# Normalised rows transposed by DMA instead of on TensorE, with stores and loads of v begun by ScalarE

## The chip, the cores and the metric

The kernel runs on one core of a Trainium2 chip. The core has five engines that work side by side, each with its own list of instructions: TensorE (PE, matrix products), VectorE (DVE), ScalarE (ACT), GpSimd (POOL) and SyncE (SP), which only begins DMA transfers. ScalarE and GpSimd can begin transfers too. The metric is the device time of one execution in microseconds (us), lower is better.

## What is computed

Attention with a causal mask and a decay from a cumulative sum of `s`, for 8 batches of 8 heads, 576 tokens and head width 64; then a layer norm over the 512 joined channels, a two-layer MLP of width 2048 with relu, and the residual sum.

```python
scores = scale * np.matmul(q, k.transpose(0, 1, 3, 2))
cum = np.cumsum(np.maximum(s, 0.0), axis=-1)
bias = -(cum[:, :, :, None] - cum[:, :, None, :])
scores = np.where(causal, -1e9, scores + np.minimum(bias, 0.0))
attn = softmax(scores)                      # over the last axis
x = np.matmul(attn, v)                      # heads joined: (8, 576, 512)
xn = (x - mean(x)) / np.sqrt(var(x) + 1e-6) * g_ln
out = x + np.maximum(xn @ w_ch1, 0.0) @ w_ch2
```

## The kernel before

The main loop runs over n = 0 to 63, one (batch, head) pair a step: b = n // 8, h = n % 8. The order of the instructions on each engine is that of the code (a manual schedule); semaphores are put in where data or a buffer is waited for.

A step n does this. `pre(n)` (L675) begins loads, casts and DMA transposes for later heads. `scores` (L304) multiplies keys by queries into three PSUM banks, and ScalarE takes the exponential of each (L323); from n = 10 on GpSimd then cuts the diagonal blocks to the causal triangle (L331). `scores_d` (L341) does the last 64 tokens for two heads at a time. `pv_next` (L729) multiplies the probabilities of the head two steps back by v (L389), and VectorE divides by the row sums (L397 to L406). Between these stand units of the MLP of the batch before: `run_units` (L557) takes them from a queue, 32 a batch. The first 16, `mlp1` (L493), make one block of 128 hidden channels each: four matmuls of 512 columns and a relu on ScalarE (L507), for the first unit of a step on VectorE (L505). The other 16, `mlp2` (L511), are quarters of the second layer for four tiles of 128 tokens; the last quarter is followed by VectorE's scaling and residual sum (L524) and a store (L542). A batch has a fifth piece, its last 64 tokens; these of two batches share a tile `xm`, and the four such tiles make a ninth, mixed set of units at the end.

Queries and keys come in two ways. For groups of four heads with a number below NPE (5 before, so heads up to 3 of batch 2) `ld_cast_pair` (L130) loads two heads by a casting DMA of GpSimd's, `qk_pair` (L275) transposes them on TensorE and VectorE and ScalarE copy them out of PSUM. Later groups are loaded as token rows: `ld_rows` (L159) in SyncE's queue, `cast_rows` (L172) on GpSimd, which also appends the bias columns, and `tr_rows` (L182), a DMA transpose in SyncE's queue. They run 6 to 2 steps ahead of the group's first head.

v of batches 2 to 7 is loaded by `ld_v` (L134, in SyncE's queue, one of five tiles a step at heads 1 to 5 of the batch before) and cast by GpSimd one step later (`cast_v`, L152). Row loads and v loads share the buffers of the pool `stage`, of which there are six.

The layer norm of a batch follows its last head, at head 1 of the next batch: `ln_xn` (L444) makes the rows minus mean times gain, `xn`, on VectorE, one tile after the other. `ln_tr` (L478) transposes a tile: four matmuls against the identity into PSUM and one copy into `xT` (or `xTm` for the mixed tile). For batches 1 to 6 that is at heads 2 and 3 of the next batch, between units. At the end of head 3 the next 32 units are queued; the first of them, at head 4, needs all four full tiles of `xT`.

SyncE's queue thus holds, in the order of the code, row loads, DMA transposes of rows, v loads and stores. Each DMA also waits until an earlier one has ended, the last that used the same one of eight semaphores.

Of the kernel before, what the change touches and what calls it, by code (L numbers as in the profile page):

```python
# [9 lines left out]
F32 = mybir.dt.float32  # L10
# [5 lines left out]
P = 128  # L16
# [3 lines left out]
def kernel(  # L20
# [25 lines left out]
    EW = 1664  # L46
    G = 4
    NG = BH // G
    NPE = 5
    NM = 10  # L50
    NR = 4
    QT = 6
    QP = S // QT

    const = ctx.enter_context(tc.tile_pool(name="const", bufs=1))
    stage = ctx.enter_context(tc.tile_pool(name="stage", bufs=6))
    pairs = ctx.enter_context(tc.tile_pool(name="pairs", bufs=4))
    small = ctx.enter_context(tc.tile_pool(name="small", bufs=4))
    xpool = ctx.enter_context(tc.tile_pool(name="xpool", bufs=3))
# [74 lines left out]
    def ld_v(b, t):  # L134
        if b >= B:
            return
        pn = P if t < NF else TL
        tmp = stage.tile([P, H, D], F32, name="vtmp", tag="st")
        nc.sync.dma_start(
            out=tmp[:pn], in_=v[b, :, t * P : t * P + pn, :].rearrange("h s d -> s h d")  # L140
        )
        loaded["v", b, t] = tmp
# [137 lines left out]

    def k_cols(b, h, kb):
        i, hh = (b * 2 + h // G) % 2, h % G
        if b * 2 + h // G < NPE:
            return kq[i][0:KA, 0, hh, kb * P : (kb + 1) * P]
        n = P if kb < NF else TL
        o = kb * 2 * G * P + hh * n
        return kq[i].rearrange("p u h s -> p (u h s)")[0:KA, o : o + P]

    def q_cols(b, h, q0, q1):
        i, hh = (b * 2 + h // G) % 2, h % G  # L290
        if b * 2 + h // G < NPE:
            return [(q0, q1, kq[i][0:KA, 1, hh, q0:q1])]
        flat = kq[i].rearrange("p u h s -> p (u h s)")
        full = flat[0:KA, 0 : NF * 2 * G * P].rearrange("p (t h s) -> p t h s", t=NF, s=P)
        o = NF * 2 * G * P + (G + hh) * TL
        got = []
        if q0 < NF * P:
            qf = min(q1, NF * P)
            got.append((q0, qf, full[:, q0 // P : qf // P, G + hh, :]))
        if q1 > NF * P:  # L300
            got.append((NF * P, q1, flat[0:KA, o : o + TL]))
        return got
# [175 lines left out]
    def ln_tr(b, t, eng="dve"):  # L478
# [9 lines left out]
            dst = xTm[:, :, (b // 2) * P : (b // 2 + 1) * P]  # L488
        copy_on(eng, dst, tr)

    first_unit = [False]

    def mlp1(xT, fb):  # L493
# [45 lines left out]
    def batch_units(b):  # L539
        def of_t(t):  # L540
            def put(yo, c0, c1):
                nc.sync.dma_start(out=out[b, t * P : (t + 1) * P, c0:c1], in_=yo)  # L542
            return xb[b][:, t, :], rstd[:, b, t : t + 1], put
        return chunk_units(lambda: xTs[b], of_t)

# [7 lines left out]

    queue = []
    pend = []

    def run_units(n, dve_first=False):  # L557
        for i in range(n):
            if queue:
                first_unit[0] = dve_first and i == 0  # L560
                queue.pop(0)()

# [103 lines left out]

    PAIR_LOADS = {11: 8, 12: 9}
    PAIRS = {9: 5, 11: 6, 13: 7, 14: 8, 15: 9}


    def pre(n):  # L675
        if n == 0:
            nc.vector.memset(mhalf, -0.5)
            ld_cast_pair(4)
        elif n == 1:
            ld_w1(1)  # L680
        elif n == 3:
            ld_cast_pair(5)
            for t in range(NT):
                ld_cast_v(1, t)
        elif n == 4:
            ld_w1(2)
            ld_w1(3)
        elif n == 7:
            ld_cast_pair(6)
            ld_w2(0)  # L690
            ld_cast_pair(7)
            ld_w2(1)
        elif n == 10:
            ld_w2(2)
            ld_w2(3)
        elif n == 12:
            nc.vector.memset(cT[:, :, 0, :, 0], -1.0)
            nc.vector.memset(cT[:, :, 1, :, 1:4], 1.0)
        elif n == 14:
            for r in rows:  # L700
                nc.gpsimd.memset(r[:, :, :, KA:P], 0.0)
        if n in PAIR_LOADS:
            ld_cast_pair(PAIR_LOADS[n])
        if n % 4 == 0 and 2 <= n // 4 + 1 < NPE:
            aug(n // 4 + 1, nc.sync)
        for gam in range(NPE, NG):
            m = n - 4 * gam
            if m == -6:
                ld_rows(gam, 0), ld_rows(gam, 1)
            elif m == -5:  # L710
                cast_rows(gam, 0), cast_rows(gam, 1)
                ld_rows(gam, 2), ld_rows(gam, 3)
            elif m == -4:
                tr_rows(gam, 0), tr_rows(gam, 1)
                cast_rows(gam, 2), cast_rows(gam, 3)
                ld_rows(gam, 4)
            elif m == -3:
                tr_rows(gam, 2), tr_rows(gam, 3)
                cast_rows(gam, 4)
            elif m == -2:  # L720
                tr_rows(gam, 4)
        for nb in range(2, B):
            m = n - H * nb + (5 if nb == 2 else 7)
            if 0 <= m < NT:
                ld_v(nb, m)
            if 1 <= m <= NT:
                cast_v(nb, m - 1, "pool")
# [17 lines left out]
    for n in range(BH):  # L745
        b, h = n // H, n % H
        pre(n)
        if n < 8:
            scores(b, h)
            if h in (1, 3, 5, 6):  # L750
                scores_d(b, h // 2)
            if h in (0, 2, 4):
                qk_pair(h // 2 + 1, ("dve", "dve"), ("act", "dve" if h < 4 else "act"))
            pend.append((b, h))
            if n == 7:
                pv_next()
                tr_pair(4)
                pv_next()
                evac_pair("k", 4, ("act", "act"))
                evac_pair("q", 4, ("act", "act"))  # L760
                trc = bias_tr()
                keep_warm(8)
                continue
            if n % 2 == 1 or n == 0:
                keep_warm(2)
            if n > 1:
                pv_next()
            if n == 6:
                pv_next()
            continue  # L770
        if n == 8:

            phs = [
                pool.tile([P, 512], F32, name="ph", tag=tag)
                for pool, tag in ((ps_m, "m"), (ps_m, "m"), (ps_s, "s"), (ps_s, "s"))
            ]

            def columns(t):
                cols = slice(t * P, (t + 1) * P)
                for fb, ph in enumerate(phs):  # L780
                    for kd in range(KD):
                        nc.tensor.matmul(
                            ph[:, cols],
                            lhsT=w1_bf[:, kd, fb * P : (fb + 1) * P],
                            rhs=xTs[0][:, kd, cols],
                            start=(kd == 0),
                            stop=(kd == KD - 1),
                        )

            for t in range(NF):  # L790
                ln_tr(0, t, "act" if t < 3 else "dve")
                if t > 0:
                    columns(t - 1)
            columns(NF - 1)
            for fb, ph in enumerate(phs):
                if fb % 2 == 0:
                    nc.scalar.activation(out=hT[:, fb, :], in_=ph, func=ACT.Relu)
                else:
                    nc.vector.tensor_scalar_max(out=hT[:, fb, :], in0=ph, scalar1=0.0)
            ln_first_rstd()  # L800
            queue += batch_units(0)[4:]
            scores(b, h)
            scores_d(b, h // 2)
            pend.append((b, h))
            run_units(1)
            continue

        end = next(m for m in (8 * i + 3 for i in range(2, B + 1)) if m >= n)
        nu = (2 if n < 16 else -(-len(queue) // (end - n + 1))) - 2
        if n in PAIRS:  # L810
            qk_pair(PAIRS[n], ("dve", "dve"), ("act", "act"))
        scores(b, h)
        run_units(1, True)
        if h % 2 == 0:
            scores_d(b, h // 2)
        run_units(1)
        if n > 9:
            pv_next()
        if n == 9:
            bias_rows(trc)  # L820
        pend.append((b, h))
        lt = {2: (0, 1), 3: (2, 3, 4)}.get(h, ()) if b > 1 else ()
        for t in lt:
            ln_tr(b - 1, t, "act" if b == 2 else "dve")
            if t != 1 and t != 4:
                run_units(1)
                nu -= 1
        if n == 2 * H + 2:
            for t in range(3, NT):
                ln_xn(1, t)  # L830
        run_units(nu)
        if b > 1 and h == 3:
            run_units(len(queue))
            queue += batch_units(b - 1)
# [4 lines left out]
    for t in range(NT):  # L839
        ln_xn(B - 1, t + 1)  # L840
        run_units(1)
        ln_tr(B - 1, t, "act")
    run_units(len(queue))
    queue += batch_units(B - 1)
    queue += mixed_units()
# [30 lines left out]
```

The softmax here doesn't subtract the row's maximum and nothing guards it: scores larger than these inputs give would overflow.

## Time and profile before

| | |
|---|---|
| runs, median of three | 367.6 us (367.05 to 368.54) |
| the profiled execution | 368.54 us, its span 366.8 us |
| transposes of xn on TensorE (L484) | 144 instructions, of which 16 for batch 0 |
| DMA transposes of rows (L186) | 55 in SyncE's queue |
| v loads, row loads, stores in SyncE's queue | 30, 110 and 37 |
| DMA traffic | 52.17 MB in 156653 packets, 143641 of them under 512 bytes |
| idle time of GpSimd until a row load has landed (L176) | 46.0 us |

How to read it: the span is the time from the first to the last instruction; the execution takes 1.7 us more. A row of the page in 40 slices gives the busy share of an engine in tenths. In rows of the timeline the columns are the start (us), the length (us), engine, line, operation, what is written and read, and the count of merged instructions; brackets hold the idle time before and what ended it. "SPq" is SyncE's queue: the length is that of beginning the DMA, not of the transfer. Ends of matmuls are modelled, so their cost is best read from start to start.

### The profile page before, as it was taken

How to read it: one execution, taken by the hardware profiler on the slowest of the kernel's cores; microseconds unless marked ns; L12 is line 12 of the kernel's file. 1: busy time of each engine (PE TensorE's matmuls, PEld its weight loads, DVE VectorE, ACT ScalarE, POOL GpSimd, SP SyncE). 2: the span in 40 equal slices, each digit the busy share in tenths (PEclk: the TensorE clock that was granted, in tenths of full speed). 3: DMA queues.
4: the chain of work that ended last, by engine and by line, in shares of the span. 5: the costliest groups of instructions: out<-in, count | busy, mean ns of one | idle time of the engine just before them, and what ended most of it. 6: DMA issues, size and time to landing. Idle time of an engine off the chain costs nothing.

```text
span 366.8 us, 8315 instructions
## 1 busy us (share of the span) xinstructions
PE 355.0 (97%) x3017; PEld 197.1 (54%) x3067; DVE 202.9 (55%) x535; ACT 191.3 (52%) x367; POOL 164.9 (45%) x447
## 2 busy tenths in 40 slices
PE   8998999999999999999999999999999999999995
PEld 3677555565555555555455555555555554444444
DVE  7697789684357554944384547743675483112211
ACT  5895988467732673367534753476337522501410
POOL 8854468667633656344675563554852101000000
PEclk9999999999999999999999999999999999999999
DMA  8999999999965999599979986798830011011013
GB/s 144 162 195 178 202 211 193 163 240 176 183 146 141 206 199 181 104 215 163 188 176 213 194 183 140 189 191 182 174 102 2 0 59 57 1 58 59 0 31 86
DMA packets 156653, 52.17 MB, mean 142 GB/s; under 512 B 143641, under 2 KB 151940, under 8 KB 156612
## 3 DMA queue, kind: packets, MB, share of 16 engines
q1 hardware_dynamic: 138868, 43.08, 55.5%
q0 software_dynamic: 17344, 8.03, 18.9%
q8 instruction: 24, 0.39, 0.5%
q10 hardware_dynamic: 400, 0.52, 0.4%
q14 instruction: 17, 0.14, 0.2%
HBM read 37.11 MB, written 9.44 MB: 127 GB/s over the span
## 4 chain that ended last, share of the span: by engine, by line
PE 72%; DVE 7%; DMA 6%; SPq 4%; POOL 4%; issue 3%; ACT 3%; POOLq 0%; ACTq 0%
PE py L515 26%; PE ph L497 25%; PE pot L389 6%; SPq L164 3%; PE sc L312 3%; PE sa L312 3%; PE sb L312 3%; DMA rowtmp<-in_q_dram 2%; PE idle L568 2%; DMA vtmp<-in_v_dram 2%; DVE xn L451 2%; PE trx L484 2%; DVE stats L423 1%; POOL er L331 1%; ACT er L323 1%
## 5 line engine op out<-in xcount | busy, mean ns | idle before, releaser
L515 PE MATMUL py<-w_bf,hT 128*128 128x512 bf16 (+1 forms) x565 | 132.1, 373 | 1.6 <-DVE yo L524 0.4
L497 PE MATMUL ph<-xT,w_bf 128*128 128x512 bf16 x478 | 116.4, 379 | 1.1 <-DVE yo L524 0.2
L507 ACT ACTIVATE hT<-ph 128x512 bf16<-128x512 f32 x102 | 61.0, 598 | 64.4 <-PE ph L497 64.4
L515 PEld LDWEIGHTS <-hT 128*128 128x128 bf16 x592 | 53.5, 98 | 49.1 <-issue 0.9
L497 PEld LDWEIGHTS <-w_bf 128*128 128x128 bf16 x560 | 50.1, 97 | 51.3 <-issue 2.9
L323 ACT ACTIVATE er<-sa 128x512 bf16<-128x512 f32 x64 | 38.2, 597 | 70.9 <-PE sa L312 50.1
L331 POOL TENSOR_SCALAR_AFFINE_SELECT er<-er 128x128 bf16<-128x128 bf16 x216 | 59.7, 300 | 22.5 <-ACT er L323 22.3
L505 DVE TENSOR_SCALAR hT<-ph 128x512 bf16<-128x512 f32 x38 | 26.3, 692 | 56.7 <-PE ph L497 49.0
L176 POOL CAST rows<-rowtmp 128x512 bf16<-128x512 f32 (+1 forms) x55 | 33.5, 609 | 50.7 <-DMA rowtmp<-in_q_dram 46.0
L312 PEld LDWEIGHTS <-kq 68*128 68x128 bf16 x452 | 33.4, 97 | 27.4 <-issue 1.7
L389 PEld LDWEIGHTS <-er 128*128 128x128 bf16 x960 | 37.5, 98 | 14.9 <-issue 0.7
L389 PE MATMUL pot<-v_bf,er 128*128 128x65 bf16 x960 | 40.2, 193 | 0.5 <-PE sd L355 0.3
L397 DVE RECIPROCAL rinv<-pot 128x5 f32<-128x5 f32 x64 | 12.3, 192 | 49.2 <-PE pot L389 48.9
L323 ACT ACTIVATE er<-sc 128x512 bf16<-128x512 f32 x64 | 39.2, 612 | 0.0
L323 ACT ACTIVATE er<-sb 128x512 bf16<-128x512 f32 x64 | 38.4, 599 | 0.3 <-PE sb L312 0.2
L524 DVE SCALAR_TENSOR_TENSOR yo<-py,rstd,xb 128x512 f32<-128x512 f32 x32 | 23.9, 748 | 26.2 <-PE py L515 19.7
L399 DVE TENSOR_TENSOR xb<-pot,rinv 128x256 f32<-128x256 f32 x64 | 27.2, 425 | 2.2
L102 POOL CAST v_bf<-vtmp 128x512 bf16<-128x512 f32 (+1 forms) x30 | 18.5, 617 | 19.6 <-DMA vtmp<-in_v_dram 19.5
L439 POOL TENSOR_TENSOR rstd<-rstd,mhalf 128x4 f32<-128x4 f32 (+1 forms) x8 | 8.8, 1095 | 38.0 <-DVE rstd L438 37.9
L312 PE MATMUL sc<-kq 68*128 68x256 bf16 (+1 forms) x216 | 25.3, 229 | 0.3
L423 DVE BATCH_NORM_STATS2 stats<-xb 128x6 f32<-128x128 f32 (+2 forms) x100 | 25.3, 313 | 0.4
L312 PE MATMUL sb<-kq 68*128 68x64 bf16 (+1 forms) x172 | 24.5, 244 | 0.9 <-DMA kq<-rows 0.6
(101 smaller groups left out, 322.1 us busy)
## 6 DMA issues: line engine op xcount, KB each, us to landing
out_dram<-yo SPq DMA_DIRECT2D x32, 256.0 KB
vtmp<-in_v_dram SPq DMA_DIRECT2D x24, 256.0 KB
rowtmp<-in_k_dram SPq DMA_DIRECT2D x44, 128.0 KB
rowtmp<-in_q_dram SPq DMA_DIRECT2D x44, 128.0 KB
w_bf<-in_moe_w_ch_dram POOLq DMA_DIRECT2D x8, 512.0 KB, 10.7
kp<-in_k_dram POOLq DMA_DIRECT2D x9, 144.0 KB, 6.8
qp<-in_q_dram POOLq DMA_DIRECT2D x9, 144.0 KB, 7.0
v_bf<-in_v_dram POOLq DMA_DIRECT2D x8, 128.0 KB, 8.1
```

The costliest lines, as they stand in the source:

```text
L176: nc.gpsimd.tensor_copy(out=r[0:pn, :, :, 0:D], in_=loaded.pop(("rows", gam, t))[0:pn])
L312: nc.tensor.matmul(a[:, c + a0 - q0 : c + a1 - q0], lhsT=k_cols(b, h, kb), rhs=cols, start=True, stop=not (pe_mask and diag),)
L323: nc.scalar.activation(out=e[:, o : o + 512], in_=a, func=ACT.Exp, scale=scale)
L331: nc.gpsimd.affine_select(out=e[:, o : o + P], in_=e[:, o : o + P], compare_op=ALU.is_ge, fill=0.0, base=0, pattern=[[1, P]], channel_mult ...
L389: nc.tensor.matmul(pot[:, t, :], lhsT=e[:, o : o + P], rhs=vv[:, kb, h, :], start=(kb == 0), stop=(kb == last),)
L399: nc.vector.tensor_tensor(out=xb[b][:, :, hs], in0=pot[:, 0:NF, 0:D], in1=rinv[:, 0:NF].unsqueeze(2).to_broadcast([P, NF, D]), op=ALU.mult,)
L423: nc.vector.bn_stats(out=st[b][:, t, part, :], in_=x[:, lo:hi])
L497: nc.tensor.matmul(ph, lhsT=w1_bf[:, kd, fb * P : (fb + 1) * P], rhs=xT[:, kd, :], start=(kd == 0), stop=(kd == KD - 1),)
L505: nc.vector.tensor_scalar_max(out=hT[:, fb, :], in0=ph, scalar1=0.0)
L507: nc.scalar.activation(out=hT[:, fb, :], in_=ph, func=ACT.Relu)
L515: nc.tensor.matmul(py[0], lhsT=hT[:, fb, t * P : (t + 1) * P], rhs=w2_bf[:, fb, c0:c1], start=(fb == 0), stop=(fb == FB - 1),)
L524: nc.vector.scalar_tensor_tensor(out=yo, in0=py[0], scalar=rs, in1=x[:, c0:c1], op0=ALU.mult, op1=ALU.add)
```

## The change

- Batches 1 to 7: the transposes of `xn` leave TensorE. `ln_dma` begins a DMA transpose in SyncE's queue for each tile: in `pre`, at head 2 of the next batch for the four full tiles and at head 5 for the mixed one; for batch 1 three at n = 18 and two at n = 19; for batch 7 in the loop after the last head, where `ln_tr` was. The four tiles of batch 0 stay on TensorE.
- NPE now counts batches: 3, so that heads 4 to 7 of batch 2 (group 5, before token rows) come as pairs 10 and 11, transposed on TensorE at n = 16 and n = 21.
- v loads are begun by ScalarE, into two buffers of their own; `stage` has four instead of six.
- Stores of full tiles are begun by ScalarE, after the unit that follows the one that made them.

```diff
-    NPE = 5
+    NPE = 3
...
-    stage = ctx.enter_context(tc.tile_pool(name="stage", bufs=6))
+    stage = ctx.enter_context(tc.tile_pool(name="stage", bufs=4))
...
-        tmp = stage.tile([P, H, D], F32, name="vtmp", tag="st")
-        nc.sync.dma_start(
+        tmp = stage.tile([P, H, D], F32, name="vtmp", tag="v", bufs=2)
+        nc.scalar.dma_start(
             out=tmp[:pn], in_=v[b, :, t * P : t * P + pn, :].rearrange("h s d -> s h d")
         )
...
-        if b * 2 + h // G < NPE:
+        if b < NPE:
...
+    def ln_dma(b, t):
+        if (b, t) not in xns:
+            return
+        if t < NF:
+            dst = xTs[b][:, :, t * P : (t + 1) * P]
+        else:
+            dst = xTm[:, :, (b // 2) * P : (b // 2 + 1) * P]
+        nc.sync.dma_start_transpose(out=dst, in_=xns.pop((b, t)))
...
             def put(yo, c0, c1):
-                nc.sync.dma_start(out=out[b, t * P : (t + 1) * P, c0:c1], in_=yo)
+                stores.append((out[b, t * P : (t + 1) * P, c0:c1], yo))
...
                 first_unit[0] = dve_first and i == 0
+                held = list(stores)
+                stores.clear()
                 queue.pop(0)()
+                for dst, src in held:
+                    nc.scalar.dma_start(out=dst, in_=src)
...
-    PAIR_LOADS = {11: 8, 12: 9}
-    PAIRS = {9: 5, 11: 6, 13: 7, 14: 8, 15: 9}
+    PAIR_LOADS = {11: 8, 12: 9, 13: 10, 16: 11}
+    PAIRS = {9: 5, 11: 6, 13: 7, 14: 8, 15: 9, 16: 10, 21: 11}
...
-        if n % 4 == 0 and 2 <= n // 4 + 1 < NPE:
+        if n % 4 == 0 and 2 <= n // 4 + 1 < 2 * NPE:
             aug(n // 4 + 1, nc.sync)
-        for gam in range(NPE, NG):
+        for gam in range(2 * NPE, NG):
+            m = n - 4 * gam
+            if m == -2:
+                tr_rows(gam, 4)
+        if n > 16 and n % H == 2:
+            for t in range(NF if n > 18 else 3):
+                ln_dma(n // H - 1, t)
+        if n == 19:
+            ln_dma(1, 3), ln_dma(1, 4)
+        if n > 19 and n % H == 5:
+            ln_dma(n // H - 1, 4)
+        for gam in range(2 * NPE, NG):
...
-        lt = {2: (0, 1), 3: (2, 3, 4)}.get(h, ()) if b > 1 else ()
-        for t in lt:
-            ln_tr(b - 1, t, "act" if b == 2 else "dve")
-            if t != 1 and t != 4:
-                run_units(1)
-                nu -= 1
...
         run_units(1)
-        ln_tr(B - 1, t, "act")
+        ln_dma(B - 1, t)
```

More of the change, by code (lines that the diff above doesn't have):

```diff
@@ L290, in q_cols @@
         i, hh = (b * 2 + h // G) % 2, h % G
-        if b * 2 + h // G < NPE:
+        if b < NPE:
             return [(q0, q1, kq[i][0:KA, 1, hh, q0:q1])]
@@ L555 @@
     pend = []
+    stores = []
     def run_units(n, dve_first=False):
@@ L698, in pre @@
             nc.vector.memset(cT[:, :, 1, :, 1:4], 1.0)
-        elif n == 14:
+        elif n == 16:
             for r in rows:
@@ L719, in pre @@
                 cast_rows(gam, 4)
-            elif m == -2:
-                tr_rows(gam, 4)
         for nb in range(2, B):
```

## The prediction

> **What bounds the kernel now.** I read the page first (busy shares and the 40 slices), then the groups of instructions by shape, then the instructions in order of time engine by engine. From the page:
>
> ```profile
> PE 355.0 (97%) x3017; PEld 197.1 (54%) x3067; DVE 202.9 (55%) x535; ACT 191.3 (52%) x367; POOL 164.9 (45%) x447
> ...
> PE   8998999999999999999999999999999999999995
> ...
> DMA  8999999999965999599979986798830011011013
> ```
>
> TensorE is full from the second slice on. A full row can hide slow instructions, so I priced the work by start to start times, here where the tiles of batch 3 are transposed (start, us, engine, line, operation, count):
>
> ```profile
> 154.22 0.39 PE L484 MATMUL trx<-ident,xn 128*128 128x128 bf16 x4
> 154.45 1.03 PE L515 MATMUL py<-w_bf,hT 128*128 128x512 bf16 x4
> 155.31 0.39 PE L484 MATMUL trx<-ident,xn 128*128 128x128 bf16 x4
> 155.54 0.81 PE L515 MATMUL py<-w_bf,hT 128*128 128x512 bf16 x3
> ```
>
> Four matmuls of 512 columns follow each other in 0.86 us (154.45 to 155.31), with no hole: TensorE is the bound here, and four transposes cost it 0.23 us. The DMA row is nearly as full for three quarters of the span, and SyncE's queue and GpSimd stand behind it. So I followed one batch through the other engines, at head 4 of batch 3, where the first MLP units of the next batch start. ScalarE, then GpSimd, then SyncE's queue:
>
> ```profile
> 118.78 0.60 ACT L323 ACTIVATE er<-sa 128x512 bf16<-128x512 f32 x1 [3.45 <-PE sa L312]
> ...
> 120.95 0.60 ACT L507 ACTIVATE hT<-ph 128x512 bf16<-128x512 f32 x1 [0.46 <-PE ph L497]
> ```
>
> ```profile
> 117.69 0.61 POOL L176 CAST rows<-rowtmp 128x512 bf16<-128x512 f32 x1 [2.70 <-DMA rowtmp<-in_q_dram]
> ...
> 119.59 0.61 POOL L176 CAST rows<-rowtmp 128x512 bf16<-128x512 f32 x1 [1.14 <-DMA rowtmp<-in_q_dram]
> 120.15 0.21 POOL L177 COPY rows<-cT 128x32 bf16<-128x32 bf16 x1
> 120.31 0.62 POOL L102 CAST v_bf<-vtmp 128x512 bf16<-128x512 f32 x1
> ```
>
> ```profile
> 112.77 0.36 SPq L542 DMA_DIRECT2D out_dram<-yo  x1
> 113.22 1.24 SPq L186 DMA_TRANSPOSE kq<-rows  x1
> 114.51 0.57 SPq L164 DMA_DIRECT2D rowtmp<-in_k_dram  x1
> ```
>
> The reader should see two things. GpSimd runs late: the cast of v's tile 1, written in the code one head earlier, ends at 120.93, 2.15 us after ScalarE began the exponentials of head 4. Nobody on TensorE's path waits for that today. And SyncE's row loads at 114.51 stood behind a store that waited for VectorE (112.77).
>
> **What the Trainium skill says.** Perfetto Trace Analysis, section "DMA Instruction — HWDGE (DVE, Sync)", has a DMA's semaphore wait happen on the issuing sequencer, before the next instruction is read; "DVE / Act Engine Instruction" has compute instructions pushed to a queue, after which the sequencer goes on. So a load on ScalarE that must wait for a buffer holds every exponential behind it, while one that needn't wait can be issued beside running activations. The trace agrees for SyncE (the store above held the rows behind it); for ScalarE no DMA stands among activations in the kernel before. DMA: Bandwidth & Descriptors, "Issuing engines are not separate DMA queues": the queues share the same 16 engines, so moving a DMA saves issue time only. No run here shows that yet. VectorE: DVE Perf Modes, "The three transpose paths", gives 1309 ns for a DMA transpose of 128x128. Here the measured issue is 1260 ns for 128x1024, eight such blocks, so the measurement decides.
>
> ```profile
> L186 SPq DMA_TRANSPOSE kq<-rows x55: 1215/1260/2791, 61.2 to 267.5; - x55
> ```
>
> **The change part by part.** The sum is made against the profiled execution, 368.54 us (span 366.8, 1.7 outside); it lies 0.9 above the median, 367.6.
>
> Removed from TensorE: 4 or 5 tiles in each of batches 1 to 7, 32 tiles, by 0.23 us: -7.4 us. They lie in stretches without holes, the last five too, so the whole sum is on the path. Their 32 copies out of PSUM (0.42 us on VectorE, 0.59 on ScalarE) are off it.
>
> Added on TensorE: two pairs (10 and 11) by 12 transposes, start to start 0.51 us a pair (52.14 to 52.65): +1.0. Their copies, 0.80 us each, four on VectorE and four on ScalarE: pair 10 falls at head 16, where ScalarE idles 2 to 3 us a head: nothing. Pair 11 falls at head 21, an MLP stage with three relus: 1.6 us ahead of that head's exponentials against a slack of 0.85 (below): I take 1.0, bounds 0 and 2.
>
> Group 5's path as token rows goes: 10 loads, 5 transposes and 10 casts and copies, all off the path. The one visible stall on transposed rows, TensorE at 176.94 where 176.17 would do, should go with the freer SyncE queue: -0.8.
>
> SyncE: per batch about 4 stores and 5 v loads leave it (0.36 and 0.59 us each, 4.4 us), 4 or 5 transposes of 128x512 come. The trace shows no such size; the 64-row ones take 1215 ns, so the time doesn't go by rows but perhaps by 128-column blocks: 4 of 8 gives 0.65 us (2.9 us a batch); if it is fixed, 1.26 (5.7). I take 0.65, keep 1.26. The transposes wait for VectorE's rows, and row loads for the next group are queued behind them. The last row is ready at 112.00, so the loads start near 112.65 instead of 114.51. The MLP first needs xT about 118, so a landing 2 to 3 us after issue (the rows above landed so) is covered. In batch 1 the fourth tile is made only at 78.65 for a use near 80: nothing taken, up to 1.5.
>
> ScalarE takes 30 v loads and 32 stores. An issue of 0.4 to 0.6 us without a wait hides in its idle time, except at heads 11 to 15, where it works through: 5 loads by 0.5, half of it beside queued activations: +1.0, bounds 0 and 2.7. A store waits for VectorE's sum, but in the second half of the MLP, where TensorE needs no relu: nothing.
>
> The v loads wait too. Their own pool has two buffers, so the load of tile 3, at head 4 just ahead of the exponentials, waits for GpSimd's cast of tile 1, behind the row casts shown above. Behind it stand three exponentials and the relu of the second unit; TensorE's fourth unit needs that relu's PSUM buffer. The slack is 0.46 idle before the relu at 120.95 plus about 0.4 from its end, 121.55, to the fourth unit near 122.0: 0.85 us. For batches 2 to 6 the exponentials began at 81.51, 118.78, 157.10, 196.53, 234.85; the casts ended at 83.02, 120.93, 161.67, 199.27, 238.52, of which 0.40, 0.85 and 0.73 in the last three was a wait for v's own load, now begun earlier. Lags: 1.5, 2.15, 4.2, 1.9, 2.9. To each: the gain from earlier row loads (0, 1.9, 2.9, 1.9, 3.0; the first is held by the rstd chain, not by loads), TensorE's earlier arrival (4 or 5 tiles, 0.9 or 1.15), the issue 0.5. ScalarE is late by 3.2, 1.7, 2.9, 1.4, 1.6; minus 0.85: 2.3, 0.85, 2.05, 0.5, 0.7 = +6.4. With 1.26 us transposes, starting when the first row is ready (2.8 us before the last), the loads start 1.6 us later in four batches: 12.8. Below it is bounded by 0, if GpSimd has caught up.
>
> DMA engines: 32 transposes of 128 KB come, group 5's 1.2 MB of transposes and 1.2 MB of narrow loads go; v's 256 KB now runs beside the row loads that GpSimd waits for. I take +1.0, bounds 0 and 2.5.
>
> Sum: -7.4 + 1.0 + 1.0 - 0.8 + 1.0 + 6.4 + 1.0 = +2.2, so 370.7 against 368.54, and 369.8 on the scale of the median; I say 370.0. All lower bounds give 361.4, all upper ones 382.
>
> **Rivals.** *The waits don't come true* (faster). If SyncE, rid of stores and loads, starts the rows early and they land without delay, GpSimd's cast of tile 1 ends before ScalarE reaches head 4. Speaking for it: in three of five batches the estimated stall is under 1 us, the size of my errors. Against: batches 2 and 4 have lags that no earlier load removes. Then -7.4 + 1.0 - 0.8 and at most 1.5 of small losses: 361 to 364. It decides at 1.3 us a batch: if all five stalls together are under 4.2 us, the change gains.
>
> *SyncE's transposes are slow* (much slower). At 1.26 us each, or with landings that delay xT past head 4, stalls double: +6.4 by the sum above, and up to 1.5 a batch for xT: 375 to 382. For it: SyncE is issuing or waiting most of the time already, and DMA shows nines. Against: the issue time measured doesn't depend on bytes, and 4.4 us a batch leave the queue.
>
> **How the numbers follow.** Forecast case (its own range 366 to 374): 0.56, of which 0.12 lies within 0.5% (1.8 us, what measurement can tell from no change). Waits don't come true: 0.27, of which 0.05 within. Slow transposes: 0.17. Faster 0.22, same 0.17, slower 0.44 + 0.17 = 0.61. The range 362 to 378 leaves out the ends of both rivals.
>
> **What would show it.** Right: no trx on TensorE after batch 0; at head 4 of batches 2 to 6, a hole of 0.5 to 2.5 us before a ph matmul, ScalarE's idle time there ending with GpSimd's v cast; rows loaded 2 to 3 us earlier after the last xn. Wrong: those holes absent (faster rival); transposes near 1.2 us in SyncE's queue, or TensorE waiting for xT (slow rival). The forecast fails most easily in the lags, since each is a difference of two times on engines that both move.

## The result, and the profile after

The changed kernel takes 397.05 us (median of 4, 391.64 to 400.97) against 367.33 us before (366.91 to 368.54): ratio 1.0754, 95% interval 1.0643 to 1.0865. It is slower, and by far more than forecast. The execution of 400.97 us fell in a slow state and is left out of the ratio, which compares the means of the others. The profiled execution is the quickest one, 391.64 us with a span of 389.4; its mean granted TensorE clock (1 is full speed) is 0.973, and two others, of 396.80 and 397.29 us, had 0.960 and 0.955. So part of what follows, the clock above all, is larger in the median than in the trace.

From the page of the changed kernel: busy times of the engines, then busy tenths in 40 slices.

```profile
PE 357.7 (92%) x2904; PEld 193.5 (50%) x2951; DVE 197.3 (51%) x517; ACT 188.8 (48%) x361; POOL 161.9 (42%) x441
...
PE   8998988959999699969997999969999999999995
...
PEclk9999999987999999999999699978999999999999
DMA  8999992699985999499969979698832005002002
```

The row of nines of before has holes at regular distances, one a batch, and behind some of them the clock row falls to 6 to 8 tenths. What TensorE waited for (us in total, times, the longest):

```profile
PE ph L507 <- ACT hT L517: 12.9, 5, 3.4
PE ph L507 <- DMA xT<-xn: 4.7, 2, 4.3
```

All rows of this view together give 24.3 us; for the kernel before they give 4.6. The hole of batch 3, and that of batch 5 with what follows it, in TensorE's timeline (start, length, engine, line, operation, count, idle time before and what ended it):

```profile
133.69 1.02 PE L507 MATMUL ph<-xT,w_bf 128*128 128x512 bf16 x4 [3.03 <-ACT hT L517]
...
214.75 1.86 PE L507 MATMUL ph<-xT,w_bf 128*128 128x512 bf16 x4 [2.89 <-ACT hT L517]
216.41 0.63 PE L312 MATMUL sa<-kq 68*128 68x512 bf16 x1
216.84 0.63 PE L312 MATMUL sb<-kq 68*128 68x64 bf16 x3
```

After the second hole four matmuls take 1.66 us from start to start (214.75 to 216.41), where four took 0.86 before: the clock is at one half. After the first they take 0.86, though that hole is the longer one. The trace's record of the granted clock tells why. In all 20 traces of this case the clock changes only at points of a grid of 3.41 us, which begins at another place in each trace. In the changed kernel it falls three times between start and end, at 84.71, 214.41 and 258.79, each time for 6.83 us. Here are cells of that grid around the holes of batches 3, 5 and 6 (busy us and counts of PE, PEld, DVE, ACT, POOL, then PEclk, DMA share, GB/s):

```profile
129.08:132.49 3.41, 1.53 (x20) 0.84 (x19) 0.99 (x4) 1.05 (x3) 2.97 (x10) 1.00 1.23 271
132.49:135.91 3.42, 2.22 (x16) 1.19 (x16) 0.00 (x0) 2.59 (x7) 2.73 (x10) 1.00 1.17 237
211.00:214.41 3.41, 0.86 (x4) 0.29 (x3) 0.91 (x3) 1.91 (x5) 3.41 (x12) 1.00 1.17 213
214.41:221.24 6.83, 6.26 (x22) 2.62 (x23) 0.69 (x1) 2.95 (x6) 3.86 (x13) 0.50 1.25 207
255.37:258.79 3.42, 0.37 (x2) 0.09 (x1) 0.38 (x2) 1.95 (x5) 3.30 (x11) 1.00 1.31 209
258.79:265.61 6.82, 6.52 (x23) 2.72 (x23) 0.69 (x1) 2.90 (x6) 4.27 (x16) 0.50 1.16 233
```

The hole of batch 3 lies across a grid line, so TensorE is idle for 1.88 us in one cell and 1.20 in the next, and the clock stays. Those of batches 5 and 6 leave it idle for 2.55 and 3.05 us in one cell, and the clock falls at the end of that cell. Over the 20 traces there are 32 such falls, all after a cell with at least 1.6 us idle; above 1.95 us it always fell, and between the two values it did both (ends of matmuls are modelled, so the limit is known no better). A fall of 6.83 us at half clock costs up to 3.4 us of work.

Now head 4 of batch 3, the place shown of the kernel before, on ScalarE, GpSimd and in SyncE's queue:

```profile
131.02 0.38 ACTq L139 DMA_DIRECT2D vtmp<-in_v_dram  x1
131.44 0.60 ACT L323 ACTIVATE er<-sa 128x512 bf16<-128x512 f32 x1 [6.87 <-POOL er L331]
...
133.04 1.08 ACT L517 ACTIVATE hT<-ph 128x512 bf16<-128x512 f32 x2
```

```profile
128.45 0.61 POOL L176 CAST rows<-rowtmp 128x512 bf16<-128x512 f32 x1 [4.66 <-DMA rowtmp<-in_q_dram]
...
129.65 0.62 POOL L176 CAST rows<-rowtmp 128x512 bf16<-128x512 f32 x1 [0.44 <-DMA rowtmp<-in_k_dram]
130.21 0.21 POOL L177 COPY rows<-cT 128x32 bf16<-128x32 bf16 x1
130.37 0.62 POOL L102 CAST v_bf<-vtmp 128x512 bf16<-128x512 f32 x1
```

```profile
118.03 5.83 SPq L499 DMA_TRANSPOSE xT<-xn  x4
123.91 0.58 SPq L164 DMA_DIRECT2D rowtmp<-in_k_dram  x1
124.54 0.50 SPq L164 DMA_DIRECT2D rowtmp<-in_q_dram  x1
```

Read from the bottom up: four transposes hold SyncE's queue from 118.03 to 123.86, the row loads start behind them, land 4 us later, GpSimd casts two row tiles and then v's tile 1 (end 130.99), and in the same moment ScalarE begins the load of v's tile 3 that waited for this buffer. Its exponentials follow at 131.44, the relu at 133.04, and TensorE's fourth unit at 133.69. The page names GpSimd's L331 as the releaser; the v cast just ahead of it is the one that fits the 131.02, and in batches 4 to 6 too the load begins 0.03 to 0.04 us after the end of that cast.

A transposed tile's issue in SyncE's queue (ns: least, median, most):

```profile
L499 SPq DMA_TRANSPOSE xT<-xn x28: 1188/1217/1857, 76.7 to 325.1; - x28
L186 SPq DMA_TRANSPOSE kq<-rows x50: 1194/1271/2241, 88.0 to 280.8; - x50
```

A 128x512 transpose (1217 ns) occupies the queue about as long as one of 1024 columns (1271, with the 64-row ones among them). At head 4 of batch 2, where batch 1's `xT` is first read, the hole is of another kind, on TensorE and in SyncE's queue:

```profile
86.81 1.89 PE L507 MATMUL ph<-xT,w_bf 128*128 128x512 bf16 x4 [4.30 <-DMA xT<-xn]
```

```profile
76.72 3.97 SPq L499 DMA_TRANSPOSE xT<-xn  x3
80.74 0.57 SPq L164 DMA_DIRECT2D rowtmp<-in_k_dram  x1
...
82.52 0.51 SPq L164 DMA_DIRECT2D rowtmp<-in_q_dram  x1
83.12 1.20 SPq L499 DMA_TRANSPOSE xT<-xn  x1
```

The fourth tile's rows were ready at 81.02. Its transpose stood until 83.12 behind four row loads, which three transposes had made late, and TensorE, ready at 82.51, got the tile 3.7 us after that (86.81).

**Where the time went.** Three terms make up the difference in span: waits of TensorE, work taken from TensorE, and clock, counted as (1 - clock) x span. For the changed kernel: waits 24.3 - 4.6 = +19.7; clock 10.5 - 0.7 = +9.8; work -7.4 + 1.0 = -6.4 (the prices of the prediction; -5.2 where batch 1 stays on TensorE). That is 366.8 + 23.1 = 389.9 against a measured 389.4. The same sum on the runs below:

| profiled execution | waits | clock | work | sum | measured span |
|---|---|---|---|---|---|
| v loads alone | 15.3 | 0.991 | 0 | 380.2 | 381.4 |
| stores alone | 15.5 | 0.994 | 0 | 379.2 | 377.6 |
| transposes alone | 30.4 | 0.974 | -7.4 | 394.7 | 393.5 |
| changed, five v buffers | 20.6 | 0.987 | -6.4 | 380.6 | 380.2 |
| changed, paired transposes | 24.5 | 0.976 | -6.4 | 388.9 | 389.9 |
| cand_c | 8.4 | 0.995 | -5.2 | 366.5 | 366.1 |
| cand_a (the worst fit of all) | 14.4 | 0.995 | -5.2 | 372.5 | 375.2 |

### The profile page after: what moved, and what is told of

Read it like the earlier page. It is cut to its first block, busy times and chain, and to the rows that moved or that the text cites. A ratio compares the mean times of both kernels' runs of the same rounds, so it can differ in the third digit from the quotient of the medians.

```text
span 389.4 us, 8159 instructions
## 1 busy us (share of the span) xinstructions
PE 357.7 (92%) x2904; PEld 193.5 (50%) x2951; DVE 197.3 (51%) x517; ACT 188.8 (48%) x361; POOL 161.9 (42%) x441
## 3 DMA queue, kind: packets, MB, share of 16 engines
q10 hardware_dynamic: 33136, 16.00, 15.5%
## 4 chain that ended last, share of the span: by engine, by line
PE 66%; DVE 11%; DMA 9%; issue 5%; ACT 5%; SPq 2%; POOL 1%; ACTq 1%; POOLq 0%
PE ph L507 28%; PE py L525 22%; PE pot L389 5%; PE sc L312 3%; PE sa L312 3%; PE sb L312 2%; ACT er L323 2%; DMA xT<-xn 2%; DMA rowtmp<-in_q_dram 2%; DVE stats L423 2%; DMA rowtmp<-in_k_dram 2%; SPq L164 2%; DVE yo L534 2%; DVE xb L399 1%; DMA kq<-c 1%
## 5 line engine op out<-in xcount | busy, mean ns | idle before, releaser
L507 PE MATMUL ph<-xT,w_bf 128*128 128x512 bf16 x476 | 124.1, 395 | 18.8 <-ACT hT L517 12.9
L507 PEld LDWEIGHTS <-w_bf 128*128 128x128 bf16 x560 | 51.5, 100 | 73.6 <-issue 23.5
L331 POOL TENSOR_SCALAR_AFFINE_SELECT er<-er 128x128 bf16<-128x128 bf16 x216 | 59.0, 292 | 58.2 <-ACT er L323 57.7
L176 POOL CAST rows<-rowtmp 128x512 bf16<-128x512 f32 (+1 forms) x50 | 30.5, 609 | 40.3 <-DMA rowtmp<-in_q_dram 27.7
L312 PE MATMUL sa<-kq 68*128 68x512 bf16 x64 | 24.9, 389 | 0.6 <-DMA kq<-c 0.3
```

What stands on the lines that cost most here:

```text
L176: nc.gpsimd.tensor_copy(out=r[0:pn, :, :, 0:D], in_=loaded.pop(("rows", gam, t))[0:pn])
L312: nc.tensor.matmul(a[:, c + a0 - q0 : c + a1 - q0], lhsT=k_cols(b, h, kb), rhs=cols, start=True, stop=not (pe_mask and diag),)
L331: nc.gpsimd.affine_select(out=e[:, o : o + P], in_=e[:, o : o + P], compare_op=ALU.is_ge, fill=0.0, base=0, pattern=[[1, P]], channel_mult ...
L507: nc.tensor.matmul(ph, lhsT=w1_bf[:, kd, fb * P : (fb + 1) * P], rhs=xT[:, kd, :], start=(kd == 0), stop=(kd == KD - 1),)
```

## The experiments

All were timed against the kernel before on the same chip. Ratios are to it, with 95% intervals.

| run | median us | ratio |
|---|---|---|
| before_v_act | 383.72 | 1.0479 (1.0426 to 1.0531) |
| before_lndma | 396.29 | 1.0805 (1.0758 to 1.0851) |
| before_stores_act | 379.28 | 1.0343 (1.0293 to 1.0394) |
| after_tr_pe | 383.54 | 1.0462 (1.0433 to 1.0490) |
| after_v5 | 386.16 | 1.0503 (1.0436 to 1.0571) |
| after_v5_sp | 375.81 | 1.0239 (1.0186 to 1.0293) |
| after_v5_order | 381.09 | 1.0397 (1.0347 to 1.0446) |
| v_pool_order | 376.43 | 1.0248 (1.0225 to 1.0272) |
| after_xp | 392.36 | 1.0680 (1.0632 to 1.0728) |
| lndma_defer | 380.34 | 1.0372 (1.0346 to 1.0397) |
| before_defer | 366.82 | 0.9982 (0.9958 to 1.0006) |
| cand_a | 375.75 | 1.0229 (1.0180 to 1.0278) |
| cand_b | 381.79 | 1.0404 (1.0372 to 1.0437) |
| cand_c | 365.73 | 0.9939 (0.9914 to 0.9963) |
| cand_d | 369.03 | 1.0032 (1.0004 to 1.0060) |
| before_rp | 368.78 | 1.0041 (1.0014 to 1.0069) |
| cand_e | 364.42 | 0.9930 (0.9904 to 0.9956) |
| cand_f | 365.25 | 0.9948 (0.9922 to 0.9975) |

### One part alone, or one undone

Theory A: ScalarE's wait for a v buffer is the cost, with the clock that falls after it. Theory B: the transposes in SyncE's queue. Theory C: the stores on ScalarE.

**v loads alone** (before_v_act).

```diff
-    stage = ctx.enter_context(tc.tile_pool(name="stage", bufs=6))
+    stage = ctx.enter_context(tc.tile_pool(name="stage", bufs=4))
...
-        tmp = stage.tile([P, H, D], F32, name="vtmp", tag="st")
-        nc.sync.dma_start(
+        tmp = stage.tile([P, H, D], F32, name="vtmp", tag="v", bufs=2)
+        nc.scalar.dma_start(
```

> The kernel before with the v loads alone begun by ScalarE, into two buffers of their own (row and pair buffers four). Transposes stay on TensorE, stores on SyncE. Theory A: the wait for GpSimd's cast is there by itself, five holes of 1 to 4 us and a fallen clock: 378 to 395 us. Theories B and C: 366 to 370 us.

383.72 us, with TensorE waiting for the relu 9.3 us in five holes: theory A's wait is there without the rest of the change. (The `stage` pool shrinks here as it does in the change; that was not tried by itself.)

**Transposes alone** (before_lndma: `ln_dma` and its places in `pre`, no `ln_tr` after batch 0; stores and v stay in SyncE's queue).

> The kernel before with the DMA transposes of normalised rows alone (SyncE's queue; v loads and stores stay in it, group 5 stays as token rows). Theory A: TensorE loses 7.4 us of transposes, one wait for the fourth tile of batch 1 of 2 to 5 us comes: 361 to 370 us. Theory B: GpSimd's casts and the row loads late, holes in most batches: 385 us or more.

396.29 us: theory A as the only cause has fallen. TensorE waits for xT in every batch, 21.7 us in 7. SyncE's queue and TensorE at batch 2's transposes:

```profile
118.97 0.36 SPq L552 DMA_DIRECT2D out_dram<-yo  x1
119.42 1.23 SPq L186 DMA_TRANSPOSE kq<-rows  x1
120.70 5.19 SPq L498 DMA_TRANSPOSE xT<-xn  x4
```

```profile
127.28 1.86 PE L507 MATMUL ph<-xT,w_bf 128*128 128x512 bf16 x4 [2.85 <-DMA xT<-xn]
```

A store stands ahead of the transposes. It waits for `yo`, which VectorE makes only behind all its `xn` (end 118.94); then five transposes need 6.5 us, and TensorE comes too early.

**Stores alone** (before_stores_act: the list `stores` and its loop in `run_units`).

> The kernel before with the stores of full tiles alone begun by ScalarE, after the unit that follows. Theory C (a store on ScalarE waits for VectorE's sum, and for the SyncE transfer that last used its semaphore, and holds the exponentials behind it): 374 to 384 us, with waits of TensorE for the exponential of sd at the transposes of xn, which the changed kernel with its transposes back on TensorE showed (9.0 us in 5). Theory A alone (only v's load matters): 364 to 368 us, since SyncE no longer waits for VectorE's sum.

379.28 us, as theory C had it. ScalarE and TensorE at head 2 of batch 6:

```profile
235.04 0.34 ACTq L566 DMA_DIRECT2D out_dram<-yo  x1
235.49 0.27 ACT L358 ACTIVATE er<-sd 64x128 bf16<-64x128 f32 x1 [4.48 <-POOL rstd L439]
```

```profile
235.81 0.38 PE L484 MATMUL trx<-ident,xn 128*128 128x128 bf16 x4 [2.70 <-DVE xm L406]
```

VectorE's `yo`, late behind its `xn`, ended at 235.01; the store follows at once, and behind it the exponential of `sd` (the scores of the last 64 tokens), which ends at 235.76. Its PSUM buffer comes from the pool of TensorE's transposes, so these stop. The view names VectorE's `xm`, which ends at the same 235.76, but in the trace the matmul waits on ScalarE's semaphore.

**Changed, with the transposes back on TensorE** (after_tr_pe: `ln_tr` and its places as before, the rest as changed).

> The changed kernel with the transposes of normalised rows of batches 1 to 7 back on TensorE (v loads and stores by ScalarE, pairs 10 and 11 stay). Theory A: ScalarE's wait is still there, a little smaller since row loads start earlier: 380 to 395 us. Theory B: 366 to 371 us, holes gone.

383.54 us, inside theory A's range, but not by theory A's wait: relu waits are only 1.6 us; 9.0 us in 5 are TensorE's transposes waiting for the exponential of `sd`, the store's price again. So each of the three parts alone is slow, by 12 to 30 us, and they don't add up: the moves to ScalarE take away most of what the transposes suffer in SyncE's queue, and the transposes take away what the stores hurt.

### What is left when one wait is cured

**Five v buffers** (after_v5).

```diff
-        tmp = stage.tile([P, H, D], F32, name="vtmp", tag="v", bufs=2)
+        tmp = stage.tile([P, H, D], F32, name="vtmp", tag="v", bufs=5)
```

> The changed kernel with five v buffers instead of two, so that ScalarE's load of v's tile 3 no longer waits for GpSimd's cast of tile 1. Theory A (ScalarE's wait for a v buffer opens the holes at head 4 and the clock falls after them): 371 to 382 us; TensorE's waits for the relu (12.9 us in 5) nearly gone, only the 4.3 us wait for the transposed rows of batch 1 and its slow stretch stay. Theory B (the transposes in SyncE's queue, with the later row loads, are the cost): 390 us or more, as before this edit. Theory C (stores by ScalarE are the cost): 388 or more.

386.16 us, above theory A's range and below those of B and C: relu waits fell from 12.9 to 6.9 us, not to nothing. At head 4 of batch 6, ScalarE, then SyncE's queue:

```profile
247.58 0.36 ACTq L577 DMA_DIRECT2D out_dram<-yo  x1
248.20 1.08 ACTq L139 DMA_DIRECT2D vtmp<-in_v_dram  x1
...
249.38 0.60 ACT L323 ACTIVATE er<-sa 128x512 bf16<-128x512 f32 x1 [4.57 <-DMA rowtmp<-in_q_dram]
```

```profile
243.42 0.66 SPq L164 DMA_DIRECT2D rowtmp<-in_q_dram  x1
244.12 0.51 SPq L164 DMA_DIRECT2D rowtmp<-in_k_dram  x1
```

The v buffer was free. In the trace every DMA names the semaphore that it raises, and those begun by SyncE and ScalarE share eight. This store and this load name the ones that just these two row loads had used last. The row loads landed at 247.50 and 248.12, 4 us after they began; store and load begin 0.08 us after that, and ScalarE's exponentials behind them (theory D).

**The same, v begun by SyncE** (after_v5_sp: `nc.scalar.dma_start` of the v load back to `nc.sync.dma_start`).

> The changed kernel with v's loads back in SyncE's queue, into five buffers; the only difference from the five-buffer run is the engine that begins them. Theory D (what is left of ScalarE's lateness there is its DMAs waiting for SyncE's row loads that last used the same one of eight semaphores): fewer DMAs stand ahead of the exponentials, 378 to 384 us, the relu waits (6.9 us in 6) down to under 3. If SyncE's queue is the narrow place: 388 to 396 us, waits for xT in most batches.

375.81 us, below the range that theory D gave (so the size was missed) and 10 us better than with ScalarE; relu waits 1.3 us in 2. The wait for xT in batch 1 (5.3 us) remains.

**Batch 1's last transposes ahead of the row loads** (after_v5_order, with the five v buffers).

```diff
-        if n == 19:
-            ln_dma(1, 3), ln_dma(1, 4)
...
-                ld_rows(gam, 0), ld_rows(gam, 1)
+                if n != 18:
+                    ld_rows(gam, 0), ld_rows(gam, 1)
...
                 ln_xn(1, t)
+                ln_dma(1, t)
+            ld_rows(6, 0), ld_rows(6, 1)
```

> The changed kernel with five v buffers, and with batch 1's fourth and fifth transposes begun at the end of step 18, ahead of group 6's first row loads, which move behind them. If the wait of 5.6 us for xT in batch 1 comes from those row loads in SyncE's queue: it falls to under 2.5 us, and the time to 376 to 381 us (386.2 without this edit). If it comes from the transposes themselves: 384 us or more.

381.09 us, just above the forecast; the wait fell from 5.6 to 3.3 us, not under 2.5. The fourth tile's transpose, in SyncE's queue, and what TensorE then waited:

```profile
80.81 1.24 SPq L499 DMA_TRANSPOSE xT<-xn  x1
```

```profile
85.69 1.50 PE L507 MATMUL ph<-xT,w_bf 128*128 128x512 bf16 x4 [3.30 <-DMA xT<-xn]
```

The order of the queue is one part of the wait. The rest is the landing: the rows were ready at 80.78 and the transpose began at once, but TensorE, ready at 82.39, got the tile 4.9 us after that begin.

**v by GpSimd's casting DMA** (v_pool_order, with that order).

```diff
-            if 0 <= m < NT:
-                ld_v(nb, m)
             if 1 <= m <= NT:
-                cast_v(nb, m - 1, "pool")
+                ld_cast_v(nb, m - 1)
```

> The changed kernel with v of batches 2 to 7 loaded by GpSimd's casting DMA straight into its bfloat16 tile (no cast, no v buffer, no load on ScalarE or SyncE), and batch 1's transposes ahead of the row loads. Stores stay on ScalarE. Theories A and D: no v load stands ahead of an exponential any more, relu waits under 3 us: 364 to 372 us. If GpSimd's own issue of these loads delays its triangle cuts, or if ScalarE's stores hold the exponentials as much as the v loads did: 374 us or more.

376.43 us, the second alternative: no v load is left on ScalarE, and holes of 3.34 and 2.18 us stay in batches 4 and 6, where a store waits for a row load's semaphore (ScalarE idle 4.4 and 3.4 us until it had landed). A wait of 2.0 us for GpSimd's triangle cut has come as well.

**Two tiles to a transpose** (after_xp: `xn` in tiles of two, `xT` by token tile, all else as changed).

```diff
+        if t == NF:
+            nc.sync.dma_start_transpose(out=xTm[:, b // 2], in_=xn)
+        elif t % 2 == 1:
+            nc.sync.dma_start_transpose(
+                out=xTs[b][:, t - 1 : t + 1].rearrange("p t k s -> p (t k) s"),
+                in_=wide[b, t].rearrange("p t c -> p (t c)"),
+            )
```

> The changed kernel with one DMA transpose for two tiles of normalised rows (128x1024) instead of one each; xT lies by token tile, all else as changed, ScalarE's v loads and two buffers too. If a transpose occupies SyncE's queue for about 1.25 us whatever its width, three instead of five a batch free 2.4 us there, the row loads behind them start earlier and ScalarE's wait for GpSimd's cast shrinks: TensorE's relu waits from 12.9 us to 5 or less, 380 to 388 us. If the time goes by width, nothing changes: 392 to 400 us.

392.36 us: a miss. The issue is 1232 ns for 128x1024, so the fixed cost is real, but relu waits stay at 13.6 us, and the interval overlaps that of the changed kernel. In batch 3 row loads began 1.6 instead of 3.1 us after the last `xn`, and GpSimd's first row cast still came 7.5 instead of 7.65 us after it: landing took 5.9 instead of 4.5 us. What delays it was not settled.

### With no DMA of stores or v on ScalarE

In these runs a store enters SyncE's queue one step later, behind the transposes and loads of that step (the edit shown leaves out four `yo` buffers instead of three):

```diff
-                nc.sync.dma_start(out=out[b, t * P : (t + 1) * P, c0:c1], in_=yo)
+                stores.append((out[b, t * P : (t + 1) * P, c0:c1], yo))
...
+        for dst, src in stores:
+            nc.sync.dma_start(out=dst, in_=src)
+        stores.clear()
```

**Transposes alone, stores later** (lndma_defer) and **stores later alone** (before_defer).

> The kernel before with the DMA transposes alone, and with each store of a full tile put into SyncE's queue one step later, behind that step's transposes and loads (four yo buffers). ScalarE begins no DMA of these. If the store that waits for VectorE's sum, standing ahead of the transposes, made xT late in the run with the transposes alone (396.3 us; xT waits 21.7 us in 7): waits for xT fall under 10 us and the time to 370 to 380 us. If the transposes' own 1.2 us each and SyncE's load make xT late: 388 us or more.

> The control: the kernel before with the stores one step later in SyncE's queue and nothing else. TensorE waits for nothing there: 365 to 368 us by every theory; below 365 the later stores would be worth something by themselves.

380.34 and 366.82 us. The later store by itself changes nothing, with the transposes it is worth 16 us: waits for xT fall from 21.7 us in 7 to 5.1 in 1, and the time lands just above the forecast, since TensorE now waits 6.3 us for transposed rows.

**Stores later, v by SyncE, pairs 10 and 11 kept**, with batch 1 on TensorE (cand_a) or by DMA (cand_b).

> DMA transposes for batches 2 to 7 only, batch 1's five tiles on TensorE as before; v loads back in SyncE's queue (four own buffers), stores in SyncE's queue one step later, pairs 10 and 11 stay. ScalarE begins no DMA ahead of an exponential. Theory A with D (only ScalarE's waits and what stands ahead of the transposes cost; the DMA transposes cost TensorE nothing): 27 tiles by 0.23 us gained, 1.0 given back for the pairs: 361 to 365 us. If the transposes cost by DMA traffic or late row loads: 368 us or more.

> As the run before, but with batch 1 transposed by DMA too, its fourth and fifth tiles ahead of group 6's row loads. Expected: a wait of 1 to 3 us for xT in batch 1 and 1.2 us of transposes less: 362 to 368 us.

375.75 and 381.79 us, both forecasts missed by over 10 us. ScalarE was not the last narrow place. **Two tiles to a transpose** on top of cand_a (cand_c):

> No DMA of stores or v on ScalarE, stores one step later in SyncE's queue, batch 1 on TensorE (the 375.8 us run), now with two tiles to a DMA transpose. If SyncE's queue, filled by transposes of fixed cost, was what kept that run at 375.8 (TensorE waits there for xT 4.5 and for rows 3.2 us): both under 2 us and 364 to 370 us. If it was DMA traffic or VectorE's and GpSimd's lateness: 373 us or more.

365.73 us: faster than before, by 0.4 to 0.9%. The waits of TensorE in cand_a, then in cand_c:

```profile
PE ph L507 <- DMA xT<-xn: 4.5, 4, 1.8
PE sb L312 <- DMA kq<-rows: 3.2, 3, 1.2
```

```profile
PE py L536 <- DVE yo L545: 1.9, 2, 1.2
PE sa L312 <- DMA kq<-c: 1.4, 2, 0.8
PE sb L312 <- DMA kq<-rows: 1.4, 1, 1.4
```

No wait for xT is left. Here the queue's time was the limit. (The edit also changes the layout of `xT`, which was not tried by itself.)

**Token rows two tiles to a transpose as well** (cand_d, with three v buffers instead of four), and that alone in the kernel before (before_rp).

> As the run before, and the DMA transposes of token rows of queries and keys taken two tiles at a time too (128x2048), three instead of five a group. SyncE's queue loses another 5 us a batch if the cost is fixed: no TensorE wait on rows left, 361 to 366 us, under the kernel before. If wide transposes land later or cost by width: 370 us or more.

> The control: the kernel before with the token rows' transposes two tiles at a time and nothing else. TensorE waits there for rows 0.6 us in all: 365.5 to 368 us by every theory; if it is faster, part of any gain of the run before comes from here.

369.03 and 368.78 us: misses, the control too. The issue times of cand_d, 128x2048 and 64x1024:

```profile
L188 SPq DMA_TRANSPOSE kq<-rall x20: 1762/2786/3884, 83.0 to 263.6; - x20
L195 SPq DMA_TRANSPOSE kq<-rall x10: 1208/1251/2155, 92.9 to 267.6; - x10
```

At 2048 columns the cost is no longer fixed: 2786 ns in the median, more than two of 1024.

**cand_c without pairs 10 and 11** (cand_e, NPE = 5 as before), and with its buffers only (cand_f: five row buffers, three for v).

> The 365.7 us version (no DMA on ScalarE, stores one step later, batch 1 on TensorE, two tiles to a transpose) with pairs 10 and 11 given up again: heads 4 to 7 of batch 2 come as token rows as before; five row buffers, three for v. Its exponentials of head 16 and 24 stood 1.0 and 1.8 us behind the kernel before, where the pairs lie. If that is the pairs' cost: 363 to 365 us. If group 5's rows fill SyncE's queue in batch 2: 366 us or more, with waits for rows or xT there.

> The control: the 365.7 us version, pairs 10 and 11 kept, with five row buffers and three for v only. Nothing of the theories says that buffers are short: 364.5 to 366.5 us. If the wait on rows in batch 6 (1.4 us) came from a row buffer: up to 2 us less.

364.42 and 365.25 us, both as expected. The medians differ by 0.8 us and the intervals overlap, so the pairs' price is not settled. cand_f against cand_c (365.73) shows nothing for the buffers. Both are faster than the kernel before, cand_e by 0.4 to 1.0%.

## Why the prediction was wrong

The direction and the main mechanism were right, the sizes were not: 370.0 us (362 to 378) against 397.05. In the account above the change costs +23.1 us, where the prediction's sum was +2.2. Of the 20.9 us between them, 9.8 are the clock, for which the sum had no term, and 11.1 are waits (8.6 forecast, 19.7 found). By its steps, against the profiled execution:

- *Removed from TensorE, -7.4, pairs +1.0.* Nothing contradicts them, and the wait for transposed rows (-0.8) is gone from the view: the sum of waits, clock and work closes within 2.7 us on every run with these prices. cand_e against cand_f puts the pairs at 0.8 us, with overlapping intervals. Pair 11's copies, +1.0, cost 0.3 (at 97.72).
- *v loads at heads 11 to 15, +1.0.* TensorE's waits on copies and exponentials there are 2.0 us, the longest at 60.31 on VectorE's copies, against 0.6 before: inside the bounds.
- *The transposes' issue, 0.65 us.* Wrong: 1.22. At 0.65 they would have kept pace with VectorE's rows (0.93 us each). In batch 3 the row loads were to start 0.65 us after the last row and 1.9 earlier than before; they started 3.1 us after it (before 2.5) and took 4.5 instead of 3.2 us to the first cast. The other end, 1.26, had been kept for the range.
- *ScalarE blocked at head 4, +6.4.* The chain came out link by link, but 12.6 us large: 3.0, 3.4, 2.9 and 3.4 in batches 3 to 6 where 0.85, 2.05, 0.5 and 0.7 stood. This is mostly the row loads' start and their landing; how much of the landing is traffic (+1.0 in the sum) was not separated. In batch 2 (2.3 forecast) TensorE was itself late, and there was no such wait. So the upper bound of 12.8 for slow transposes is met in the sum by luck in part, not batch by batch.
- *Batch 1's fourth tile, 0, at most 1.5.* It cost 4.3. The slack was about as thought, 1.5 us from the rows to TensorE's need. But 2.1 us went in SyncE's queue, which the prediction left out, and 3.7 from the transpose's begin to TensorE's start, where it took a landing of 2 to 3. With the queue free (after_v5_order) the landing alone still cost 3.3.
- *The sum has no term for the clock.* This is the step that failed most plainly: +9.8 us in the profiled execution, more in the median, none of it in any of the bounds. Each of five holes was priced at its length only. Three falls of 6.83 us at half clock are 10.2 us, nearly all of the 10.5 counted. The clocks of the two other executions named above, 0.955 and 0.960, would be about five such falls (an estimate by the same count, no trace of them was kept). The rival of slow transposes (375 to 382) had their cost right and missed the time for the same reason.
- *Stores at nothing.* In the changed kernel TensorE waits for none in the second half of the MLP, as said. But the reason is that `trx` is gone: alone the stores cost 12 us. Their waits on row loads' semaphores were overlooked; after_v5 and v_pool_order show them once the buffer wait is cured.
- *The faster rival* would have needed all stalls under 4.2 us. They were three times that (12.9).

Open: why the clock stayed low for one cell of the grid after some falls and for two after others, whether matmuls that fill a hole would keep it up (not tried), why in after_xp the rows land later, and whether stores begun by GpSimd would do.

## What to carry to other kernels

A DMA begun by a compute engine brings every wait of that DMA into the engine's order: its data, its buffer, and the earlier transfer whose semaphore it takes. Before moving issues, count what each queue holds per batch and what stands ahead of the first thing that the next stage needs; here stores put a step later were worth 16 us once the transposes stood in the same queue, and two tiles to a transpose 10 after that (in the changed kernel itself the gain was not clear). When TensorE is full, price a new hole at more than its length, because the clock after it can fall: here holes that filled about half of a 3.41 us cell cost up to 3.4 us more, and which holes do so changes with where the grid lies.

## What the hardware showed

- The granted clock fell after some holes and not after others of like length: in the changed kernel after 2.89 us (four matmuls then 1.66 us), not after 3.03. What decided was the idle time inside one cell of a grid of 3.41 us: 2.55 us for the first, at most 1.88 for the second; in 20 traces all 32 falls followed a cell with 1.6 us idle or more. The Trainium skill, TensorE: Matmul & The Clock Gate, "What's actually happening", has the clock halve after an idle window of about 3.4 us that runs freely, and rise again after a busy one. The half (1.66 against 0.86 us), the length and the free running agree. How idle a window must be that section doesn't say; here 31 of the 32 were idle in part only, so a hole shorter than the window can be enough.
- A DMA transpose occupied SyncE's queue 1.22 us at 128x512 (median), 1.23 at 128x1024 (after_xp), 2.79 and 2.89 at 128x2048 (cand_d, before_rp). In the changed kernel the 32 of normalised rows landed 2.3 to 4.8 us after their begin.
- DMAs begun by SyncE and by ScalarE shared eight semaphores in this program, and one waited until the earlier transfer on its semaphore had landed, also across the two engines: ScalarE's exponentials stood 4.57 us for SyncE's row loads (after_v5).
- A load of v was begun by ScalarE in 0.39 us (median of 30, most of 256 KB; SyncE 0.59 before), beside running activations when it waited for nothing.
